# Reordering the opening of a fused FFT-filter and ELU kernel: weight fetches, table loads and on-chip weight conversion in another order

**Chip, cores, metric.** One core of one Trainium2 chip. The metric is the device time of one execution in microseconds (us); most executions of a kernel agree within 0.3%, which here is 8 us.

## The reference

```python
batch, seq, dim = (8, 3008, 256)
X = np.fft.rfft(x, axis=1)                        # x: 8 x 3008 x 256
y = np.fft.irfft(X * (filt_r + 1j * filt_i)[None], n=seq, axis=1)
h = y.reshape(24064, 256) @ w_in                  # 256 x 2048
g = np.where(h > 0, h, np.exp(np.minimum(h, 0)) - 1)
out = g @ w_out                                   # 2048 x 256
```

The weights reach the kernel as 64-bit floats. TensorE needs 32-bit ones, so the kernel converts them on the chip, in 16 pieces ("weights 0 to 15") of 0.52 MB each.

## The kernel before

The transforms are products with tables in three stages. In the kernel's words: `a_first` is the first stage on a chunk of x; `t_first` transposes; `b_unit` is the second stage of a frequency group and multiplies by the filter (four products on VectorE, lines 309 to 312); `bi_unit` is the first inverse stage, whose two results ScalarE copies (lines 329 and 330); `y_write` and `y_read` carry them through DRAM; `n_unit` is the last inverse stage (line 360), and `combine` (line 383) makes from it the operands of the first matrix product. After that the main part runs: 192 "quads" (8 batches x 6 blocks x 4 quarters of the hidden layer) on TensorE, each of two halves, with the FFT of the next batch woven in through a `plan` that hangs a function onto a half-quad. Only batch 0 has its FFT ahead of the main part, and so do the weights: that is the opening.

A weight is converted by two VectorE operations (`w_split`), four ScalarE operations (`w_float`), and three or four VectorE operations (`w_join`), every second time with four more that form sums.

```python
def w_split(k):
    m, e, c = wtmp[k % 2]                       # two sets of buffers
    ...
    nc.vector.tensor_scalar(out=m, in0=hi, scalar1=0x000FFFFF, ..., op0=ALU.bitwise_and)
    nc.vector.tensor_scalar(out=e, in0=hi, scalar1=0x7FF00000, ..., op0=ALU.bitwise_and)

def w_float(k):
    nc.scalar.activation(out=l, in_=wds[k][:, :, 0], func=AXT.Identity, ...)
    nc.scalar.activation(out=f, in_=m, func=AXT.Identity, ...)
    nc.scalar.activation(out=ef, in_=e, func=AXT.Relu, ...)
    nc.scalar.activation(out=e, in_=ef, func=AXT.Relu, ...)

# ---- the opening; NXC = 6 chunks of x, NG = 8 groups ----
TICKS = {0: 8, 1: 9, 3: 10, 5: 11, 7: 12, 8: 13, 9: 14}
f_arrange()                        # GpSimd's queue: filters rearranged, DRAM to DRAM
w_fetch(0, nc.sync)                # SyncE's queue
...
for c in range(NXC):
    x_load_first(c)                # SyncE's queue: chunk and its table
    if 0 < c < 5:
        w_fetch(c, nc.sync)
...
def tick(k):
    w_float(k)
    w_join(k - 1)

for c in range(NXC):
    w_split(c); w_float(c)
    a_first(c)
    if c > 0:
        w_join(c - 1)
        w_fetch(c + 4, nc.sync if c < 4 else nc.gpsimd)
nc.sync.dma_start(gs, gs_d)
for g in range(NG):
    f_read(0, g, ff[:, g])         # GpSimd's queue: filters to SBUF
    if g % 2:
        w_fetch(NXC + 4 + g // 2)  # w_fetch without a queue: GpSimd's
for g in range(4):
    t_first(g)
for k in (NXC, NXC + 1):
    w_split(k); tick(k); w_fetch(k + 8)
tn_read(0, 0)
for g in range(NG + 2):            # "the loop"
    k = TICKS.get(g)
    if k: w_split(k)
    if 2 <= g < NG - 2: t_first(g + 2)
    if g >= 2: bi_unit(0, g - 2)
    if g < NG: b_unit(0, g, ff[:, g], ...)
    if g >= 2: y_write(0, g - 2, (nc.sync, nc.scalar if g == NG + 1 else nc.sync))
    if g == NG + 1: y_read(0, 0, (nc.sync, nc.scalar))
    if k: tick(k)
w_split(15); tick(15)
w_join(15)
...
n_unit(0, 0)
# ---- main part: ----
for f in fbufs:                    # three filter buffers cleared together
    at(4, 1, nc.vector.memset, f, 0.0)
```

## Time and profile before

| | before |
|---|---|
| time, median of 4 runs | 2666.57 us (2664.87 to 2666.93) |
| profiled execution, span | 2665.7 us |
| TensorE busy | 2601.9 us (98%) |
| TensorE without work | 63.8 us: 51.2 up to `combine`, 4.3 in four waits behind it, 8.3 behind the last matmul |
| last chunk of x reaches TensorE | 46.3 us |
| first filter product (VectorE) | 62.8 us |
| first block enters the main part (`combine`) | 123.3 us |

The main part is the same work in both kernels and TensorE fills it. So the table to read is that of milestones in the opening. The lines are in the prediction.

The timeline of the kernel before, columns: start, length in us, engine, line, operation, tiles, idle time ahead of it and what ended it.

```profile
26.84 0.59 POOL L564 DMA_DIRECT2D wd<-in_moe_w_in_dram  x1 [0.37 <-issue]
31.69 0.55 POOL L564 DMA_DIRECT2D wd<-in_moe_w_in_dram  x1 [4.26 <-PE psa L250]
```

They are the fetches of weights 8 and 9, which start on GpSimd's queue while chunks of x are still on their way on SyncE's.

### The profile page before, as it was taken

What the parts mean: (1) busy time and instruction counts of PE and PEld (TensorE: products, weight loads), DVE (VectorE), ACT (ScalarE), POOL (GpSimd) and SP (SyncE); (2) the same over time, 40 slices, a digit from 0 to 9 for tenths busy, and PEclk for the clock granted to TensorE, in tenths of its full rate; (3) what the DMA queues carried; (4) which work ended last, traced back from release to release, by engine and by line L of the source; (5) the groups of instructions that cost most, each with busy time, mean ns of one, the idle gap of its engine ahead of it and who ended that gap; (6) DMA issues with size and microseconds to landing.
All of it is one profiled execution on the core that took longest, in us unless ns stands there. A gap on an engine that the chain in (4) does not pass through costs nothing.

```text
span 2665.7 us, 37335 instructions
## 1 busy us (share of the span) xinstructions
PE 2601.9 (98%) x13508; PEld 2213.2 (83%) x13508; DVE 1843.9 (69%) x3203; ACT 1507.8 (57%) x2622; POOL 235.6 (9%) x295
## 2 busy tenths in 40 slices
PE   4799999999999999999999999999999999999998
PEld 3388889888898878988889878898789888899887
DVE  4876767767676776767766776676767677666766
ACT  5555555555555555555555555555555555555554
POOL 4000200012000120002100021000210012000000
PEclk7799999999999999999999999999999999999999
DMA  9533411343124231333314242133421233110010
GB/s 277 129 94 92 109 44 38 92 107 94 38 51 123 77 86 38 86 97 80 78 41 102 73 99 74 38 85 96 105 56 38 68 87 87 39 40 19 21 28 17
DMA packets 224712, 202.85 MB, mean 76 GB/s; under 512 B 127586, under 2 KB 191090, under 8 KB 224528
## 3 DMA queue, kind: packets, MB, share of 16 engines
q1 hardware_dynamic: 212064, 167.23, 25.1%
q0 software_dynamic: 11008, 32.52, 4.7%
q8 instruction: 107, 1.75, 0.3%
q10 hardware_dynamic: 1456, 0.72, 0.1%
q14 instruction: 77, 0.63, 0.1%
HBM read 128.52 MB, written 74.97 MB: 76 GB/s over the span
## 4 chain that ended last, share of the span: by engine, by line
PE 95%; DMA 2%; DVE 1%; issue 0%; ACT 0%; SPq 0%; DVEq 0%; ACTq 0%
PE po L490 43%; PE phs L408 25%; PE phd L408 12%; PE pha L408 6%; PE psn L360 3%; PE pva L297 2%; PE psr L297 2%; PE psa L209 2%; DMA f<-in_moe_w_in_dram 1%; DMA xc<-in_x_dram 1%; PE pvb L297 1%; DMA wd<-in_moe_w_out_dram 0%; PE psi L297 0%; PE po L269 0%; DMA t<-yd 0%
## 5 line engine op out<-in xcount | busy, mean ns | idle before, releaser
L490 PE MATMUL po<-g,wo 128*128 128x256 f32 (+1 forms) x5376 | 1296.7, 375 | 0.0
L490 PEld LDWEIGHTS po<-g,wo 128*128 128x128 f32 x5376 | 1015.0, 190 | 129.5 <-issue 16.2
L419 ACT ACTIVATE g<-phs 128x512 f32<-128x512 f32 (+1 forms) x576 | 338.9, 588 | 844.2 <-PE phs L408 843.6
L416 DVE TENSOR_TENSOR g<-phd,g 128x512 f32<-128x512 f32 (+1 forms) x384 | 259.6, 676 | 463.7 <-ACT e L426 278.0
L426 ACT ACTIVATE e<-e 128x512 f32<-128x512 f32 (+1 forms) x768 | 477.3, 621 | 24.4
L408 PE MATMUL phs<-y,wi 128*128 128x256 f32 (+1 forms) x1536 | 395.1, 380 | 0.0
L408 PE MATMUL phs<-ys,wi 128*128 128x256 f32 (+1 forms) x1536 | 387.6, 375 | 2.5 <-ACT g L419 1.5
L430 DVE SCALAR_TENSOR_TENSOR g<-e,g 128x512 f32<-128x512 f32 (+1 forms) x576 | 387.1, 672 | 0.2 <-ACT e L426 0.2
L425 ACT ACTIVATE e<-g 128x512 f32<-128x512 f32 (+1 forms) x576 | 352.9, 613 | 35.4 <-DVE g L416 29.3
L408 PEld LDWEIGHTS phs<-y,wi 128*128 128x128 f32 x1536 | 284.9, 190 | 83.2 <-ACT t L329 34.1
L408 PEld LDWEIGHTS phs<-ys,wi 128*128 128x128 f32 x1536 | 291.4, 190 | 36.4 <-ACT g L419 2.2
L430 DVE SCALAR_TENSOR_TENSOR g<-e,phs 128x512 f32<-128x512 f32 (+1 forms) x192 | 130.0, 677 | 139.2 <-ACT e L426 139.2
L408 PE MATMUL phd<-ys,wi 128*128 128x256 f32 (+1 forms) x768 | 193.9, 375 | 1.8 <-DVE g L416 1.8
L408 PE MATMUL pha<-y,wi 128*128 128x256 f32 (+1 forms) x768 | 193.7, 375 | 0.0
L408 PE MATMUL phd<-y,wi 128*128 128x256 f32 (+1 forms) x768 | 193.7, 375 | 0.0
L425 ACT ACTIVATE e<-phs 128x512 f32<-128x512 f32 (+1 forms) x192 | 112.9, 588 | 141.4 <-PE phs L408 140.6
L318 POOL TENSOR_TENSOR sr<-sr,sp 128x512 f32<-128x512 f32 x56 | 71.1, 1270 | 1256.2 <-DVE sp L311 1256.2
L408 PEld LDWEIGHTS phd<-ys,wi 128*128 128x128 f32 x768 | 145.7, 190 | 18.9 <-DVE g L416 2.5
L408 PEld LDWEIGHTS pha<-y,wi 128*128 128x128 f32 x768 | 145.8, 190 | 16.5
L408 PEld LDWEIGHTS phd<-y,wi 128*128 128x128 f32 x768 | 145.8, 190 | 16.5
L467 DVE TENSOR_TENSOR g<-g,g 128x512 f32<-128x512 f32 (+1 forms) x192 | 130.7, 681 | 6.6
L470 DVE TENSOR_TENSOR g<-g,g 128x512 f32<-128x512 f32 (+1 forms) x192 | 130.7, 681 | 6.7
(134 smaller groups left out, 2393.1 us busy)
## 6 DMA issues: line engine op xcount, KB each, us to landing
yd<-t SPq DMA_DIRECT2D x127, 192.0 KB
t<-yd SPq DMA_DIRECT2D x190, 128.0 KB
z<-t SPq DMA_DIRECT2D x84, 256.0 KB
f<-fd POOLq DMA_DIRECT2D x112, 192.0 KB, 3.6
t<-z SPq DMA_DIRECT2D x224, 96.0 KB
out_dram<-o SPq DMA_DIRECT2D x632, 32.0 KB
tn<-tn_t SPq DMA_DIRECT2D x48, 256.0 KB
xc<-in_x_dram SPq DMA_DIRECT2D x84, 128.0 KB
```

Of the source, the lines that this page charges most:

```text
L297: nc.tensor.matmul(ps[:, u:u + w, :], table[k, v, :], r[k, u:u + w, :], start=n == 0, stop=n == len(rhs) - 1)
L318: nc.gpsimd.tensor_tensor(out=sr, in0=sr, in1=p, op=ALU.add)
L360: nc.tensor.matmul(ps[:, ts(q, P)], t[:, i - 4 * m, ds(dh * P, P)], w[:, i - 4 * m, :], start=True, stop=True)
L408: nc.tensor.matmul(ps[:, a, 0:h], w_in[q][:, COMBO[n], a, :], y[n], start=start and a == 0, stop=True, skip_group_check=True)
L416: nc.vector.tensor_tensor(out=g[o], in0=i0, in1=i1, op=ALU.add)
L419: nc.scalar.activation(out=g[o], in_=i0, func=AXT.Copy)
L425: nc.scalar.activation(out=e, in_=src, func=AXT.Relu, scale=-1.0)
L426: nc.scalar.activation(out=e, in_=e, func=AXT.Exp, scale=-1.0)
L430: nc.vector.scalar_tensor_tensor(out=g[n], in0=es[n], scalar=1.0, in1=src, op0=ALU.subtract, op1=ALU.max)
L467: nc.vector.tensor_tensor(out=b12, in0=b22, in1=b12, op=ALU.subtract)
L470: nc.vector.tensor_tensor(out=g["t4"], in0=g["b21"], in1=g["t2"], op=ALU.subtract)
L490: nc.tensor.matmul(po[i][:, u, 0:h], w_out[q][:, COMBO[n], a, :], g[n][:, a, :], start=q == 0 and a == 0 and n in (1, 3, 6, 4), stop=True, ...
```

## The change

The intent: x and the filters should not compete with weights that are needed late, and a conversion should never stand ahead of a filter product on VectorE or of the last copies on ScalarE. So:

- weights 1 to 3 go first on GpSimd's queue, ahead of the filter rearrangement; SyncE's queue carries only weights 0, 4 and 5 up to x's last chunk, and the tables (`once`, `gs`) follow x at once;
- no weight leaves on GpSimd's queue between the rearrangement and the first filter reads;
- a conversion (`step`) follows a step's products instead of framing them;
- `w_float(12)` is issued behind the last two pairs of copies;
- weight 15 is converted within the first three quads of the main part;
- the three clears are spread over quads 3 to 5.

```diff
-        elif k in (6, 7, 8, 9, 15):
+        elif k in (6, 7, 8, 9):                      # weight 15 in a filter buffer
...
-        if j % 2 == 1:
-            w = (w_in if j < 2 else w_out)[q]
+        if j % 2 == 1 and k < 15:
+            w_sums(k)                                # the four sums, cut out as a function
...
+            for k in (1, 2, 3):
+                w_fetch(k)
             f_arrange()
             w_fetch(0, nc.sync)
...
-            for c in range(NXC):
+            for c in range(3):
                 x_load_first(c)
-                if 0 < c < 5:
-                    w_fetch(c, nc.sync)
+            w_fetch(4, nc.sync)
...
+            def step(k):
+                w_split(k)
+                w_float(k)
+                if k > 0:
+                    w_join(k - 1)
+
+            for k in range(3):
+                step(k)
+            w_fetch(5, nc.sync)
+            for c in range(3, NXC):
+                x_load_first(c)
             nc.sync.dma_start(once, once_d)
-            def tick(k): ...
-            for c in range(NXC): ...
-            nc.sync.dma_start(gs, gs_d)
+            nc.sync.dma_start(gs, gs_d)
+            a_first(0)
+            w_fetch(6, nc.sync)
+            step(3)
+            for c in (1, 2):
+                a_first(c)
+                w_fetch(c + 6, nc.sync)
+            step(4)
+            a_first(3)
+            w_fetch(9, nc.sync)
+            step(5)
+            for c in (4, 5):
+                a_first(c)
+            tn_read(0, 0)
             for g in range(NG):
                 f_read(0, g, ff[:, g])
-                if g % 2:
-                    w_fetch(NXC + 4 + g // 2)
+                if 3 <= g < 5:
+                    w_fetch(g + 7)
+            for k in (12, 13):
+                w_fetch(k)
             for g in range(4):
                 t_first(g)
-            for k in (NXC, NXC + 1): ...
             for g in range(NG + 2):
-                k = TICKS.get(g)
-                if k:
-                    w_split(k)
...
-                if k:
-                    tick(k)
-            w_split(15)
-            tick(15)
-        w_join(15)
+                if g < 6:
+                    step(g + 6)
+                    if g == 0:
+                        w_fetch(14)
+                if g == 7:
+                    w_join(11)
+                    w_split(12)
+            w_float(12)
+            y_read(0, 0, (nc.sync, nc.scalar))
+            step(13)
+            w_fetch(15)
+            step(14)
+        w_join(14)
...
+        for quad, place, fn in ((0, 0, w_split), (0, 1, w_float), (1, 1, w_join), (2, 1, w_sums)):
+            at(quad, place, fn, 15)
...
-        for f in fbufs:
-            at(4, 1, nc.vector.memset, f, 0.0)
+        for i, f in enumerate(fbufs):
+            at(3 + i, 1, nc.vector.memset, f, 0.0)
```

More of the change, by code (lines that the diff above doesn't have):

```diff
@@ L552, in w_fetch @@
             wd = t1p.tile([P, XC, D], FP32, tag="t1", name="wd").rearrange("p u d -> p (u d)")
-        elif k in (6, 7, 8, 9, 15):
+        elif k in (6, 7, 8, 9):
             wd = xp.tile([P, 2, 2, D], FP32, tag="xc", name="wd").rearrange("p k u d -> p (k u d)")
         else:
-            wd = fbufs[{5: 0, 12: 1, 13: 2, 14: 0}.get(k, k)].rearrange("p c u d -> p (c u d)")
+            wd = fbufs[{5: 0, 12: 1, 13: 2, 14: 0, 15: 1}.get(k, k)].rearrange("p c u d -> p (c u d)")
         wd = wds[k] = wd.bitcast(U32).rearrange("p (a w) -> p a w", w=2)
@@ L571, in w_split @@
     def w_split(k):
-        m, e, c = wtmp[k % 2]
+        m, e, c = wtmp[k % 2 if k < 15 else 0]
         f, l = c[:, 0], c[:, 1]
@@ L606, in w_join, with w_sums @@
                 nc.vector.tensor_tensor(out=dst[:, i], in0=f[:, i], in1=e[:, i], op=ALU.mult)
-        if j % 2 == 1:
-            w = (w_in if j < 2 else w_out)[q]
-            a11, a21, a12, a22, s1, s2, s4 = (w[:, i] for i in range(7))
-            nc.vector.tensor_tensor(out=s1, in0=a21, in1=a22, op=ALU.add)
-            nc.vector.tensor_tensor(out=s2, in0=s1, in1=a11, op=ALU.subtract)
-            nc.vector.tensor_tensor(out=s4, in0=a12, in1=s2, op=ALU.subtract)
-            nc.vector.tensor_tensor(out=a21, in0=a11, in1=a21, op=ALU.subtract)
+        if j % 2 == 1 and k < 15:
+            w_sums(k)
+    def w_sums(k):
+        q, j = divmod(k, 4)
+        w = (w_in if j < 2 else w_out)[q]
+        a11, a21, a12, a22, s1, s2, s4 = (w[:, i] for i in range(7))
+        nc.vector.tensor_tensor(out=s1, in0=a21, in1=a22, op=ALU.add)
+        nc.vector.tensor_tensor(out=s2, in0=s1, in1=a11, op=ALU.subtract)
+        nc.vector.tensor_tensor(out=s4, in0=a12, in1=s2, op=ALU.subtract)
+        nc.vector.tensor_tensor(out=a21, in0=a11, in1=a21, op=ALU.subtract)
     def f_arrange():
@@ L634 @@
     with tc.manual_schedule():
-        TICKS = {0: 8, 1: 9, 3: 10, 5: 11, 7: 12, 8: 13, 9: 14}
         with tc.tile_pool(name="boot", bufs=1) as bp:
@@ L663 @@
                 nc.vector.memset(edges[:, i:i + 1], v)
-            nc.sync.dma_start(once, once_d)
-            def tick(k):
-                w_float(k)
-                w_join(k - 1)
-            for c in range(NXC):
-                w_split(c)
-                w_float(c)
-                a_first(c)
-                if c > 0:
-                    w_join(c - 1)
-                    w_fetch(c + 4, nc.sync if c < 4 else nc.gpsimd)
-            nc.sync.dma_start(gs, gs_d)
+            def step(k):
[8 more added lines that the diff above has]
+                x_load_first(c)
+            nc.sync.dma_start(once, once_d)
+            nc.sync.dma_start(gs, gs_d)
[3 more added lines that the diff above has]
+            for c in (1, 2):
+                a_first(c)
+                w_fetch(c + 6, nc.sync)
[6 more added lines that the diff above has]
+            tn_read(0, 0)
             for g in range(NG):
                 f_read(0, g, ff[:, g])
-                if g % 2:
-                    w_fetch(NXC + 4 + g // 2)
+                if 3 <= g < 5:
+                    w_fetch(g + 7)
+            for k in (12, 13):
+                w_fetch(k)
             for g in range(4):
                 t_first(g)
-            for k in (NXC, NXC + 1):
-                w_split(k)
-                tick(k)
-                w_fetch(k + 8)
-            tn_read(0, 0)
             for g in range(NG + 2):
-                k = TICKS.get(g)
-                if k:
-                    w_split(k)
                 if 2 <= g < NG - 2:
@@ L700 @@
                     y_write(0, g - 2, (nc.sync, nc.scalar if g == NG + 1 else nc.sync))
-                if g == NG + 1:
-                    y_read(0, 0, (nc.sync, nc.scalar))
-                if k:
-                    tick(k)
-            w_split(15)
-            tick(15)
-        w_join(15)
+                if g < 6:
[11 more added lines that the diff above has]
+        w_join(14)
         for c in range(2):
```

## The prediction

> **What bounds the kernel now.** I read the page's slices first, then a table of busy time by stretch, then the chain of waits and the timeline of the opening.
>
> ```profile
> PE   4799999999999999999999999999999999999998
> DMA  9533411343124231333314242133421233110010
> ...
> 0.00:57.00 57.00, 25.96 (x140) 24.00 (x144) 23.13 (x45) 30.51 (x58) 28.52 (x56) 0.73 1.01 283
> 57.00:106.00 49.00, 40.99 (x230) 16.42 (x222) 41.40 (x82) 29.58 (x52) 5.06 (x9) 0.76 0.52 131
> 106.00:118.00 12.00, 0.00 (x0) 0.00 (x0) 9.39 (x21) 6.33 (x11) 0.00 (x0) 0.61 0.47 122
> 118.00:132.00 14.00, 12.27 (x56) 10.93 (x56) 11.14 (x24) 8.06 (x16) 0.00 (x0) 0.84 0.93 215
> ...
> 400.00:2600.00 2200.00, 2200.00 (x11411) 1888.59 (x11410) 1531.93 (x2648) 1250.62 (x2172) 173.11 (x197) 1.00 0.28 69
> ```
>
> The columns of the table are length, then PE, PEld, DVE, ACT and POOL busy, granted clock, DMA share and GB/s. From 195 to 2600 us TensorE is never idle at full clock: the change doesn't touch that work. TensorE busy is 2601.9 of 2665.7 us, so all that any reordering can win is 64 us of idle time, and nearly all of it lies before 132 us. There are three stretches. Up to 57 us all 16 DMA engines are full (share 1.01). From 57 to 106 us VectorE is busy 41.4 of 49 us (filter products of the first batch, with weight conversion between them). From 106 to 118 us TensorE waits for the first batch's round trip through DRAM.
>
> ```profile
> 46.28 3.76 PE L250 MATMUL psa<-t,x 128*128 128x128 f32 x16 [7.44 <-DMA x<-in_x_dram]
> ...
> 62.83 0.68 DVE L309 TENSOR_TENSOR sr<-psr,ff 128x512 f32<-128x512 f32 x1
> ...
> 107.53 0.63 ACT L583 ACTIVATE wfl<-wm 128x512 f32<-128x512 uint32 x1 [2.16 <-DVE wm L576]
> ...
> 109.43 0.58 ACT L329 ACTIVATE t<-pva 128x512 f32<-128x512 f32 x1
> ...
> 118.17 3.75 PE L360 MATMUL psn<-tn,t 128*128 128x128 f32 x16 [12.62 <-DMA t<-yd]
> ...
> 123.34 0.38 DVE L383 TENSOR_TENSOR ys<-y 128x224 f32<-128x224 f32 x1
> ```
>
> These are the milestones. The last chunk of x arrives at 46.3. The first filter product, whose matmuls ended at about 57.7, starts only at 62.8, because the join of weight 5, all of weight 6 and the split of weight 7 are ahead of it on VectorE. The last bi_unit's matmuls end at 105.5, but ScalarE copies them at 109.4: a conversion of weight 13 stands ahead and itself waits for VectorE. The first combine of the second half starts at 123.3, behind VectorE's joins of weights 14 and 15.
>
> ```profile
> q0 software_dynamic: 3666, 9.96, 52.1%
> q1 hardware_dynamic: 4784, 9.44, 49.0%
> ...
> PE phd L408 <- DVE g L416: 1.8, 1, 1.8
> ```
>
> The first two lines are the queues in the first 70 us: GpSimd's and SyncE's transfers share the engines evenly. The third, from TensorE's waits of 118 to 300 us, is the one stall that the three clears of the filter buffers cause (at 185 to 188 us on VectorE); after 300 us there is no wait at all.
>
> **What the Trainium skill says.** "DMA: Bandwidth & Descriptors", section "Queues, rings and completion order": each DMA engine takes turns between queues that have work, packet by packet. The trace agrees (52.1% against 49.0%). Its section "Issuing engines are not separate DMA queues" says that issuing from several engines saves only issue time; so moving weights 1 to 3 to GpSimd's queue changes the order of landing and not the rate, which is 283 GB/s here. "TensorE: Matmul & The Clock Gate", Part 1: the clock is halved after an idle window of about 3.4 us and restored after a busy one. The trace agrees: the granted clock is 0.50 from 20 to 50 us, and a 48x512 matmul of line 297 takes 1.06 us near 68 us and 0.59 near 102 us. Same page, on queue depths ("Architectural detail"): ScalarE and VectorE take instructions strictly in order, as the 109.4 us copy shows.
>
> **The change part by part.** No matmul, product or weight byte is removed. What moves is this.
>
> *x earlier.* Up to x's last chunk SyncE's queue carried weights 0 to 4; now it carries 0, 4 and 5. At 0.52 MB a weight that is 1.57 MB of weights, 3.1 of x and 1.5 of tables, 6.2 MB in place of 7.3. The old 7.3 MB took 46.1 us, 158 GB/s, so x should land at 6.2/0.158 = 39 us, 7 us earlier. From its first matmul (46.28) to b_unit(0)'s first (56.2) were 10 us, so b_unit(0) could run at about 49.
>
> *Filters later.* GpSimd's queue first takes weights 1 to 3, 1.57 MB. At half of 283 GB/s that is 11 us. The filter rearrangement ended at about 33 us, when the first filter read was let go (33.55), so it now ends near 43. The first read (0.39 MB) needs 3 us at half rate and some 3 of latency: the filters are there at 49 to 52. That takes about 3 us of the 7. In return GpSimd's filter reads no longer stand behind weights 6 to 9, which waited for chunk buffers.
>
> *Products first.* With both, and no conversion ahead on VectorE, I put the first product at 52 us in place of 62.8: 11 us won.
>
> *The loop.* On VectorE a group of four products takes 2.4 us (62.83 to 65.22), a split 0.68, a join 2.0 to 2.1, and with its sums 3.7 (65.22 to 68.93). Between the first product and the last now stand six splits (4.1), joins 5 to 10 (3 x 3.7 + 3 x 2.07 = 17.3) and eight groups (19.2): 40.6 us. Before, the same stretch (62.83 to 103.4) took 40.5 with 33.6 of work and 7.0 idle for TensorE. The loop therefore carries more work now. With a conversion behind each group TensorE can prepare the next during it; of the idle time I keep 3 us. That is 43.6, so the last product ends at about 96 (before 103.4): 7.4 of the 11 us remain.
>
> *The last copies.* The last matmuls end 2.1 us after the products (105.5 - 103.4), now at 98; with nothing ahead on ScalarE the two copies end at 99.2. The way from the last copy's end (110.5) to the first matmul of n_unit (118.17) is two transfers, 7.7 us; so 106.9. From there to the combine were 5.2 us: 112.1. VectorE by itself: from 96 join 11 (3.7), splits 12 and 13 (1.4) to 101; join 12 (2.1), split 14 (0.7), join 13 (3.7) and join 14 (2.1), with ScalarE's four activations per weight (2.6 us) between, end at about 112. The two paths meet, at 112.3 against 123.3: **11 us won**.
>
> *Weight 15 and the clears.* Weight 15 moves into the first three quads of the main part. VectorE has room, but ScalarE's 2.6 us stand at the end of quad 0, ahead of the copy that quad 1's second accumulation needs. TensorE waited 0.9 us for that copy already; I charge 2 us. The clears, one to a quad now in quads 3 to 5, should save the 1.8 us stall. Net 0.2 lost.
>
> Sum: 2666.3 - 11.0 + 0.2 = 2655.5, rounded to 2656.
>
> **The rivals.** *TensorE becomes the bound of the loop.* A step costs it about 3.8 us at full clock (bi_unit 2.0, b_unit 0.9, transposes 0.9) and 7.6 at half, against some 6 us of VectorE. For it: the clock of 57 to 106 us was 0.76 on average, and every slow patch there ended in VectorE waiting for TensorE. Against: a TensorE that is the bound is busy, and warms up. All six steps cold would add 9 us (2665); half of them 4.
>
> *The filters are the bound.* If rearranging, whose transfers are small, suffers more than in proportion from starting behind the weights, the first reads land near 57 and all shifts by 5 us: 2661. For it: at most eight transfers of a queue are open, and each took about 7 us to land. Against: once x is in, GpSimd's queue has the engines nearly alone.
>
> *Hidden anyway.* VectorE's total before the main part falls only by weight 15 (3.7 us), and if every product that comes early just waits for the joins at the end, only that and idle time are won: about 4 us, 2662. Against: between the first product and the combine VectorE's work grows by one join and one split only (joins 5 to 14 in place of 7 to 15), some 3 us, and about 10 of the 60.5 us there were idle.
>
> *Better than reckoned.* x at 37, filters at 46, TensorE warm: 6 us more, 2649.
>
> **Range and chances.** The first product is uncertain by about 3 us, the loop by 4, the end by 2; together some 5, with the failures tending later. I give 2649 to 2663. Faster by over 2% would need 53 us of the 64 us of idle time in all; slower by as much would need a stall that nothing here suggests. Within 2%: 0.99.
>
> **What would show it right or wrong.** In the profile after: x's last chunk matmul at 38 to 42 us (before 46.3); first product 49 to 55, with the wait ahead of it on a filter read or on TensorE; groups of products 5.5 to 7 us apart; copies of pva directly behind the last matmuls; n_unit at 105 to 109; the combine at 110 to 115; no stall at the clears, and a wait of 2 to 3 us for a copy in quad 1. The prediction is wrong if the first product is later than 57, if the loop takes over 50 us, if joins 13 and 14 end several us after n_unit's copies, or if TensorE, idle-free before from 195 us on, shows waits there.

## The result, and the profile after

| | before | after |
|---|---|---|
| time, median of 4 runs each | 2666.57 us | 2655.38 us (2652.79 to 2656.22) |
| profiled execution, span | 2665.7 us | 2651.0 us |

The ratio is 0.9958, with a 95% interval of 0.994 to 0.9975: 0.4% less time, and 0.6 us from the predicted time. All outputs are right. A ratio here is the mean time of one kernel's runs over that of the other's runs of the same rounds, so it is not quite the ratio of the medians quoted. The profiled execution of the changed kernel happened to be the fastest of its four runs, and that of the kernel before (2667.5 us) was slower than all its four, so the traces are 14.7 us apart while the medians are 11.2 apart.

The page's slices after the change:

```profile
PE   5799999999999999999999999999999999999998
...
DMA  9534311533134321423214342134321333110010
```

The first slice (66 us) rises from 4 tenths to 5; every later slice of TensorE is as before. The table by stretch after the change (columns as in the prediction: length; PE, PEld, DVE, ACT and POOL busy; clock; DMA share; GB/s):

```profile
0.00:57.00 57.00, 30.30 (x182) 25.24 (x182) 29.87 (x58) 34.27 (x63) 31.00 (x61) 0.86 1.00 297
57.00:106.00 49.00, 35.47 (x207) 18.37 (x206) 45.21 (x92) 33.18 (x58) 4.27 (x8) 0.81 0.62 162
106.00:118.00 12.00, 8.03 (x37) 6.66 (x36) 9.79 (x19) 8.29 (x16) 0.00 (x0) 0.92 0.77 184
118.00:132.00 14.00, 14.00 (x78) 12.69 (x78) 6.15 (x11) 7.38 (x14) 0.00 (x0) 0.82 0.32 86
```

Up to 57 us TensorE now works 30.3 us instead of 26.0, at the same DMA share. From 57 to 106 it is VectorE that gained, from 41.4 to 45.2 busy microseconds. And the stretch from 106 to 118, which had no matmul at all, has 8.0 us of them: the main part has begun. Queues in the first 70 us, after the change:

```profile
q0 software_dynamic: 3856, 10.49, 52.9%
q1 hardware_dynamic: 5184, 9.70, 45.8%
```

The two queues still share the engines about evenly: in 70 us GpSimd's moved 0.5 MB more than before and SyncE's 0.3. What changed is which transfer stands where. Then the milestones, in the timeline after the change:

```profile
35.97 6.22 PE L250 MATMUL psa<-t,x 128*128 128x128 f32 x32 [2.52 <-ACT we L586]
...
47.94 0.69 DVE L309 TENSOR_TENSOR sr<-psr,ff 128x512 f32<-128x512 f32 x1 [15.12 <-DMA ff<-fd]
...
92.16 0.59 ACT L330 ACTIVATE t<-pvb 128x512 f32<-128x512 f32 x1
...
93.25 0.68 ACT L582 ACTIVATE wfl<-f 128x512 f32<-128x512 uint32 x1 [0.50 <-DVE wo L617]
...
100.17 3.76 PE L360 MATMUL psn<-tn,t 128*128 128x128 f32 x16 [8.58 <-DMA t<-yd]
...
105.00 0.39 DVE L383 TENSOR_TENSOR ys<-y 128x224 f32<-128x224 f32 x1
...
116.59 0.52 ACT L419 ACTIVATE g<-phs 128x448 f32<-128x448 f32 x1
...
117.16 1.86 PE L408 MATMUL phs<-ys,wi 128*128 128x224 f32 x4 [3.34 <-ACT g L419]
```

The last two chunks of x now form one group of 32 matmuls from 35.97 us on. The last chunk has landed by 38.0 (SyncE's queue, which waited for that transfer, goes on then), and TensorE starts on it without a wait at about 39.5. The 38.0 compares with 46.3 before, where TensorE started as the chunk landed. The first product is at 47.9, and the bracket tells what it waited for: 15.1 us, ended by a filter read. The last copy starts at 92.2, and only after it comes the conversion of weight 12 (line 582 at 93.3). `n_unit` is at 100.2 and `combine` at 105.0. The last two lines are the price: in quad 1 TensorE waits 3.34 us for a ScalarE copy (line 419), which stood behind the four conversions of weight 15. TensorE's waits from 105 us on say the same in one line (columns: total us, times, longest):

```profile
PE phs L408 <- ACT g L419: 4.0, 2, 3.3
```

The wait for the clears, 1.8 us in the kernel before, is gone.

**The balance of the pair of traces.** `combine` is 18.3 us earlier (123.34 - 105.00). From `combine` to `n_unit` of the second block there were 19.37 us before (142.71 - 123.34), and there are 24.65 after (129.65 - 105.00): 5.3 us are given back in the first two quads. The clears return 1.8. 18.3 - 5.3 + 1.8 = 14.8, against a difference of spans of 14.7. Of the 5.3, the wait is 3.34 - 0.9 = 2.4. The rest is clock: the three groups of matmuls that follow the wait took 1.86, 3.19 and 1.49 us, where the same groups take 1.02, 1.68 and 0.92 at full clock, 2.9 us less. Told by idle time, the same 14.7 us are 10.8 us less of it and 3.9 us less of TensorE's busy time (2601.9 to 2598.0 us): the work of the opening itself ran at a higher clock, 0.86 against 0.73 up to 57 us.

### The profile page after: what moved, and what is told of

It is laid out like the page before. It is cut to its first block, busy times and chain, and to the rows that moved or that the text cites. A ratio compares the mean times of both kernels' runs of the same rounds, so it can differ in the third digit from the quotient of the medians.

```text
span 2651.0 us, 37333 instructions
## 1 busy us (share of the span) xinstructions
PE 2598.0 (98%) x13508; PEld 2213.7 (84%) x13508; DVE 1843.7 (70%) x3203; ACT 1507.5 (57%) x2622; POOL 236.3 (9%) x298
## 4 chain that ended last, share of the span: by engine, by line
PE 96%; DMA 2%; DVE 0%; ACT 0%; POOL 0%; issue 0%; DVEq 0%; SPq 0%; POOLq 0%
PE po L490 43%; PE phs L408 25%; PE phd L408 12%; PE pha L408 6%; PE psn L360 3%; PE pva L297 2%; PE psr L297 2%; PE psa L209 2%; DMA fd<-in_filt_i_dram 1%; DMA ff<-fd 1%; DMA wd<-in_moe_w_out_dram 0%; DMA fd<-in_filt_r_dram 0%; PE pvb L297 0%; DMA f<-in_moe_w_out_dram 0%; DMA t<-yd 0%
```

## The experiments

Questions: Which part of the change earns the gain? Is it the order of bytes on the queues, the place of the conversions, or the putting off of weight 15? And are the 5.3 us really weight 15's? Times below are medians over 5 rounds, each with "gain", the difference of mean times to the kernel before in the same call; the kernel before was at 2666.9, 2666.7, 2668.0 and 2667.1 us (medians of 9 runs) in the four calls. The calls ran on different chips. The changed kernel itself was run only in the first (experiments 1, 4, 7 and 8), where it gained 12.7 us; the others are compared with it through the kernel before, so differences of a few us between them and the changed kernel are weaker evidence.

### 1. The changed kernel again

No edit; the baseline.

> The changed kernel once more, as the yardstick of this call. My theory: the time hangs on whether TensorE's clock drops after the 3.3 us stall in quad 1 (behind weight 15's ScalarE work) and for how long, so 2652 to 2657 us, and the stall of 3 to 4 us shows in quad 1 again. Rival: the stall was an accident of one profile; then it is missing here and the time is the same.

Measured: 2654.69 us (2652.69 to 2655.35), ratio 0.9952 (0.9939 to 0.9966), gain 12.7. The trace repeats: first product 47.7, `combine` 104.8, the wait of 3.3 us in quad 1. So the stall and the early opening belong to the kernel, not to one execution.

### 2. The changed opening alone

The changed order up to the filter reads; the loop, its end, weight 15 ahead of the main part and the clears as before.

```diff
-            for g in range(NG + 2): ...   # changed loop: products, then step(g + 6)
+            for k in (NXC, NXC + 1):
+                w_split(k); tick(k); w_fetch(k + 8)
+            for g in range(NG + 2): ...   # the old loop with its TICKS, w_split(15), tick(15)
```

> The kernel before with the changed opening alone (order of the loads and of the first five conversions); loop, end, weight 15 and clears as before. My theory: x and filters allow the first product at 47 to 48 us, conversions 6 and 7 ahead of it put it at 52 to 54 (62.8 before); from there the old loop and end take 60.5 us as before, so the combine at 113 to 115 and 2656 to 2658 us, some 9 to 10 us faster than before. Rival (the order in the loop is what pays): the first product is early, but the old loop gives it back, 2662 or more.

Measured: 2654.77 us (2654.66 to 2656.14), ratio 0.9956, gain 11.6. Timeline of this kernel:

```profile
50.40 0.69 DVE L309 TENSOR_TENSOR sr<-psr,ff 128x512 f32<-128x512 f32 x1
...
110.59 0.39 DVE L383 TENSOR_TENSOR ys<-y 128x224 f32<-128x224 f32 x1
```

`combine` comes 12.75 us earlier than before, and the time gained is 11.6. **The opening by itself brings as much as the whole change.** (The edit holds the new order of the transfers and that of the first six conversions; this run doesn't part the two.) The first product has no wait ahead of it here: it stands behind the conversions that the old loop puts first, and starts only 2.5 us later than in the changed kernel.

### 3. The changed loop and end alone

The old opening, with everything else changed.

```diff
-            for k in (1, 2, 3): w_fetch(k)
...                                        # the old order up to the filter reads,
+            for c in range(NXC): ...      # with step() for the conversions of the loop
```

> The changed kernel with the opening of before (loads and first conversions), so the changed loop, end, weight 15 and clears alone. My theory: first product at about 57 us (matmuls of b_unit at 56), 41.5 us of loop and 15.6 to the combine, so the combine at 114 (123.3 before), less the stall at weight 15 (5 us) and plus the clears (1.8): 2659 to 2662 us. With the opening alone at -9 to -10 and this at -5 to -7, the parts add to more than the whole (-11.7), because both move the same conversions out of the way of the first product. Rival (the loop is the whole of it): 2656.

Measured: 2662.89 us (2662.53 to 2666.09), ratio 0.9988 (0.9976 to 1.0001), gain 3.0. Timeline:

```profile
59.41 0.69 DVE L309 TENSOR_TENSOR sr<-psr,ff 128x512 f32<-128x512 f32 x1 [8.14 <-PE psi L297]
...
119.42 0.39 DVE L383 TENSOR_TENSOR ys<-y 128x224 f32<-128x224 f32 x1
```

The first product gains 3.4 us without any earlier data, but now waits 8.1 us for TensorE. `combine` gains 3.9, and the first two quads, with the 3.3 us stall in quad 1 (it is in this trace too), give 4.1 back (23.50 us from `combine` to `n_unit` of the second block, against 19.37); the spread clears return 1.8. That is less than the 5 to 7 us expected. Together with experiment 2: the loop and the end bring `combine` forward by another 5.6 us on top of the new opening (110.6 to 105.0), but the stall costs 5.3 of them.

### 4. Weight 15 in smaller pieces

The four ScalarE conversions of weight 15 one to a half-quad, instead of four in a row at the end of quad 0.

```diff
-        for quad, place, fn in ((0, 0, w_split), (0, 1, w_float), (1, 1, w_join), (2, 1, w_sums)):
-            at(quad, place, fn, 15)
+        for quad, place, fn, a in ((0, 0, w_split, ()), (1, 0, w_float, ((0,),)), (1, 1, w_float, ((1,),)),
+                                   (2, 0, w_float, ((2,),)), (2, 1, w_float, ((3,),)),
+                                   (3, 0, w_join, ()), (3, 1, w_sums, ())):
+            at(quad, place, fn, 15, *a)      # w_float(k, parts): only these of the four
```

> Only weight 15's four ScalarE activations are moved: one at a time, in quads 1 and 2, in place of all four at the end of quad 0; join and sums in quad 3. My theory: the stall of 3.3 us in quad 1 goes, and with it the half clock that followed it (some 2 us more), so 4 to 6 us faster than the changed kernel: 2649 to 2651. Rival (the stall is the start-up of the pipeline, which the kernel before has too, with other waits): less than 1.5 us faster.

Measured: 2650.79 us (2649.43 to 2652.13), ratio 0.9937, gain 16.3: 3.6 us better than the changed kernel, a little less than the 4 to 6 expected. The table by stretch, first of the changed kernel, then of this one:

```profile
112.00:118.00 6.00, 2.66 (x12) 2.28 (x11) 5.28 (x10) 4.87 (x9) 0.00 (x0) 0.84 0.67 154
118.00:125.00 7.00, 7.00 (x35) 5.69 (x35) 1.06 (x2) 2.18 (x5) 0.00 (x0) 0.65 0.01 2
```

```profile
112.00:118.00 6.00, 5.10 (x28) 4.75 (x27) 5.36 (x11) 3.83 (x8) 0.00 (x0) 1.00 0.93 221
118.00:125.00 7.00, 7.00 (x48) 6.21 (x47) 3.74 (x7) 5.50 (x11) 0.00 (x0) 1.00 0.39 114
```

In the changed kernel TensorE is busy 2.66 of 6 us around the wait, and then runs 7 us at a mean clock of 0.65 with 35 matmuls. In pieces, it is busy 5.10 of 6, the clock stays at 1.00, and 48 matmuls fit into the same 7 us. The wait is back at 0.9. So the cause of the loss is shown: it is the row of four conversions, and about half of its cost is the clock that drops after the wait. The traces of the two kernels are 3.3 us apart: `combine` is 1.0 later in this one (105.86 against 104.82), the first two quads return all of the 5.3 (19.37 us again, against 24.71), and a new wait of 0.8 us appears, of TensorE for the sums of weight 15, which VectorE now makes later.

### 5. Weight 15 in two pieces

Two conversions at the end of quad 0, two at the end of quad 1, to see whether a shorter wait keeps the clock.

```diff
+        for quad, place, fn, a in ((0, 0, w_split, ()), (0, 1, w_float, ((0, 1),)), (1, 1, w_float, ((2, 3),)),
+                                   (2, 1, w_join, ()), (3, 1, w_sums, ())):
```

> The changed kernel with two of weight 15's four ScalarE activations left at the end of quad 0 and two moved to the end of quad 1. It tells the stall from the slow clock that follows it. My theory: ScalarE's work ahead of the copy falls by 1.3 us and the stall from 3.3 to 2.0; too short an idle time for the clock to drop (full clock from the stall on), so 3 to 5 us faster than the changed kernel, about as much as with all four spread, 2650 to 2652. Rival (the clock would have dropped in any case, only the stall counts): 1.3 us faster, 2653.5.

Measured: 2653.26 us (2652.72 to 2655.41), ratio 0.9949, gain 13.6. The wait is 1.98 us. The table by stretch of this kernel:

```profile
112.00:118.00 6.00, 4.02 (x21) 3.44 (x20) 5.16 (x10) 5.41 (x10) 0.00 (x0) 1.00 0.83 202
118.00:125.00 7.00, 7.00 (x39) 5.78 (x39) 2.27 (x4) 2.75 (x6) 0.00 (x0) 0.76 0.02 6
```

TensorE is busy 4.02 of 6 us, and yet the clock falls, to 0.76. My theory, that a wait this short leaves the clock alone, falls; the rival is right. The Trainium skill, "TensorE: Matmul & The Clock Gate", Part 1, puts the fall at an idle window of about 3.4 us. Here a wait of 1.98 us, with TensorE busy on both sides of it, was followed by a fall, so the measurement decides. But no length of wait follows from it as a limit. The clock did not fall in the wait: it stayed at 1.00 through it (115.8 to 117.75 us) and for 1.3 us of work more, then was 0.50 for 3.4 us with TensorE busy (119.1 to 122.5). And the clears' wait of 1.8 us in the kernel before, hardly shorter, left the clock alone:

```profile
190.00:195.00 5.00, 3.19 (x16) 2.53 (x15) 4.90 (x9) 3.47 (x7) 0.89 (x2) 1.00 0.64 157
195.00:200.00 5.00, 5.00 (x33) 4.61 (x32) 4.79 (x10) 2.14 (x4) 0.00 (x0) 1.00 0.00 0
```

The same is seen in the traces of experiments 2 and 10. So waits of 0.9 and 1.8 us did no harm here, and one of 2.0, in a single trace, did.

### 6. Weight 15 ahead of the main part

The changed kernel with weight 15 converted inline, as before.

```diff
             step(14)
-        w_join(14)
+            step(15)
+        w_join(15)
```

> The changed kernel with weight 15 converted ahead of the main part, as before, and not in quads 0 to 2. My theory: the combine comes 4 to 5 us later (109 to 110: split, 2.6 us of ScalarE, join and sums), and the stall of 3.3 us in quad 1 with the slow clock after it is gone (5 us), so within 1.5 us of the changed kernel's 2655: putting weight 15 off, as it was done, won nothing. Rival (putting it off hides it): 3 us or more slower.

Measured: 2658.36 us (2654.11 to 2659.25), ratio 0.9964, gain 9.4. This is about 3 us worse than the changed kernel (12.7, but on another chip, and the ranges of the runs overlap). `combine` is at 113.87, 8.9 us later; of these 4.3 are a loop that ran later (its last group of products starts at 91.31, against 87.01), which the edit doesn't touch, and 4.6 are the conversion (22.56 us from there to `combine`, against 17.99). TensorE's waits show what comes in place of the stall:

```profile
PE phs L408 <- DVE ys L385: 3.0, 1, 3.0
PE phs L408 <- ACT y L362: 2.3, 1, 2.3
```

TensorE now waits for the operands of the first block instead. The first two quads take 22.1 us in place of 24.7, so the edit itself costs about 2 us of the 6.5 between the traces. The later loop may belong to the chip or the execution: all three traces of the changed loop on this chip (experiments 3, 6 and 9) take 44.6 to 44.7 us from first to last product, against 41.5 in both of the changed kernel's. Whether putting weight 15 off pays in spite of the stall is therefore not decided.

### 7. A conversion ahead of each step's products

In the first six steps `step(g + 6)` goes ahead of `b_unit`. This undoes one point of the intent alone.

```diff
+                if g < 6:
+                    step(g + 6)
+                    if g == 0:
+                        w_fetch(14)
                 if g < NG:
                     b_unit(0, g, ff[:, g], gf, pq if g % 2 else None)
                 if g >= 2:
                     y_write(...)
-                if g < 6:
-                    step(g + 6)
-                    if g == 0:
-                        w_fetch(14)
```

> In each of the first six steps of the loop the conversion stands ahead of the filter products and not behind them. My theory: what counts is when VectorE's work is available, not that products come first; VectorE was idle for 15.1 us up to the first filter read, so the first conversion (split 6 and join 5, 4.4 us) fits into that gap and the rest of the order is unchanged; the first product stays at 47 to 49 us, the combine comes 3 to 4.5 us earlier, total 2651. Rival (the change's intent: products first pays): the first product comes 3 to 5 us later and the total is 2656 to 2660.

Measured: 2651.15 us (2649.47 to 2653.66), ratio 0.9940, gain 15.7: 3.0 us *better* than the changed kernel. Timeline:

```profile
48.83 0.69 DVE L309 TENSOR_TENSOR sr<-psr,ff 128x512 f32<-128x512 f32 x1 [3.58 <-DMA ff<-fd]
...
82.62 0.69 DVE L309 TENSOR_TENSOR sr<-psr,ff 128x512 f32<-128x512 f32 x1 [2.62 <-PE psi L297]
...
104.28 0.38 DVE L383 TENSOR_TENSOR ys<-y 128x224 f32<-128x224 f32 x1
```

The conversion fills time in which VectorE waited for the filters anyway: the wait ahead of the first product shrinks from 15.1 us to 3.6, and the product is 0.9 us later only. "Products first" therefore does not pay at the start of the loop. But the time saved shows poorly in the milestones: TensorE's later steps do not keep up (VectorE waits 2.62 and 1.26 us for it), and `combine` is earlier by 0.5 to 0.7 us. Where the 3.0 us of time come from is not settled. The profiled pair is 1.8 us apart (2650.9 and 2649.1): 0.5 is the earlier `combine`, and 1.2 lie in the first two quads, where after the same wait of 3.3 us the half clock lasted 3.5 us in place of 6.8 (mean 0.83 against 0.65 from 118 to 125 us). Nothing in the edit explains that, and among traces with the same wait both occur (0.65 to 0.83), so this part may be chance.

### 8. Both together

The edits of 4 and 7.

> Both edits of this call together. My theory: they act in different places, so the gains add: 8 us faster than the changed kernel, 2646 to 2648. Rival for either: only the other one's gain is seen, 2650 to 2652.

Measured: 2648.11 us (2645.49 to 2650.2), ratio 0.9927 (0.9914 to 0.9939), gain 19.1. **This is the best version**: it beats the kernel before by 19 us and the changed kernel by 6.4. `combine` is at 104.61, the clock stays at 1.00 from 112 to 132 us, and TensorE's waits in quad 1 are 0.9 us or less.

### 9. A conversion ahead of the last copies

`w_float(12)` right behind `w_split(12)` in the loop, so ScalarE meets it ahead of the last two pairs of copies.

```diff
                     w_join(11)
                     w_split(12)
-            w_float(12)
+                    w_float(12)
```

> The changed kernel with weight 12's ScalarE work put ahead of the last two bi_units' copies (as a conversion stood there before). My theory: those copies wait for VectorE's split 12 (94 us) and 2.6 us of activations, 96.7 in place of 91.7 to 92.2; the round trip through DRAM starts 4 to 5 us later and the combine comes at 109 to 110 (105.0): 3 to 5 us slower than the changed kernel, 2658 to 2660. Rival (VectorE's joins end at the same time anyway, so the copies are hidden): less than 1.5 us slower.

Measured: 2663.74 us (2662.03 to 2664.85), ratio 0.9989, gain 3.1. Measured through the kernel before, it costs 8 to 10 us, where I had expected 3 to 5; the rival, that the wait is hidden, falls. Timeline:

```profile
96.87 0.63 ACT L583 ACTIVATE wfl<-wm 128x512 f32<-128x512 uint32 x1 [6.52 <-DVE wm L576]
...
115.86 0.39 DVE L383 TENSOR_TENSOR ys<-y 128x224 f32<-128x224 f32 x1
```

ScalarE stands 6.5 us in front of one conversion, because VectorE has not yet made its input, with finished matmul results behind it. The Trainium skill, "TensorE: Matmul & The Clock Gate", "Architectural detail", calls ScalarE's queue strictly first in, first out, and the trace agrees: the two pairs of copies behind it leave at 98.8 to 100.8 us in one go. The last copy ends at 100.8 instead of 92.75. Of these 8 us, 3.3 are a later loop in this execution (as in experiment 6) and 4.7 the conversion; so the edit itself costs some 6 of the 9.3 us between the traces. Then a second cost joins in: the last two writes of y take 5.7 us to land, where the last took 3.1 in the changed kernel. They leave together now, but the fetch of weight 15 (0.52 MB) also runs beside them, which in the changed kernel started after y had landed. Which of the two makes the 5.7 us is not shown.

### 10. The clears together again

```diff
-        for i, f in enumerate(fbufs):
-            at(3 + i, 1, nc.vector.memset, f, 0.0)
+        for f in fbufs:
+            at(4, 1, nc.vector.memset, f, 0.0)
```

> The changed kernel with the three clears of the filter buffers back together in quad 4. My theory: TensorE's wait of 1.8 us for VectorE in quad 4 is back, and the total is 1.5 to 2 us longer than the changed kernel's, 2656 to 2657 us. Rival: with weight 15's work no longer near, VectorE absorbs the clears and the wait is not there; total the same as the changed kernel's.

Measured: 2656.32 us (2654.34 to 2657.87), ratio 0.9957, gain 11.3. The time does not resolve it: 0 to 1.4 us worse than the changed kernel. The waits do:

```profile
PE phd L408 <- DVE g L416: 1.8, 1, 1.8
```

The same line as in the kernel before is back, with the same 1.8 us. That is all that spreading the clears is worth; the clock stays at 1.00 after this wait.

### 11. Weights 1 to 3 on SyncE's queue again

They go between the chunks of x, as before; all else stays changed. SyncE's queue then carries some 7.7 MB up to x's last chunk, more than in the kernel before.

```diff
-            for k in (1, 2, 3):
-                w_fetch(k)
...
             for c in range(3):
                 x_load_first(c)
+                w_fetch(c + 1, nc.sync)
```

> The changed kernel with weights 1 to 3 back on SyncE's queue, each behind a chunk of x, everything else as changed. My theory: 1.57 MB more ahead of x's last chunk put it at 46 to 48 us (38 in the changed kernel); filters arrive some 8 us earlier but wait; the first product at 56 to 58, all 8 to 10 us later, total 2662 to 2665. Rival (both queues share the same engines, so the queue doesn't matter): first product within 3 us of 48, total 2655 to 2658.

Measured: 2654.32 us (2652.46 to 2656.08), ratio 0.9952, gain 13.0. No difference to the changed kernel. The first product in the timeline:

```profile
48.17 0.69 DVE L309 TENSOR_TENSOR sr<-psr,ff 128x512 f32<-128x512 f32 x1 [12.22 <-PE psi L297]
```

It is 0.2 us later than in the changed kernel, and now it is TensorE that it waited for, so x, and not the filters: the filter reads are let go at 34.6 us instead of 41.8, and x's last chunk is there at 40.8 instead of 38.0. The two paths tie within about a microsecond, and which queue carries weights 1 to 3 trades one for the other. **My theory falls here**, and with it a step of the prediction: had x moved at the old 158 GB/s of its queue, it would have come at 7.7 MB / 0.158 = 49 us. It came at 40.8, at 190 GB/s. So what makes x early is not mainly how much its own queue carries; that is worth these 2.8 us.

### 12. Two weights beside x's last chunks

What is left is what runs beside x. This kernel is number 11 with weights 12 and 13 (1.05 MB), which are needed late, moved forward on GpSimd's queue to just behind the filter rearrangement. No byte is added.

```diff
             step(3)
+            for k in (12, 13):
+                w_fetch(k)
             for c in (1, 2):
...
-            for k in (12, 13):
-                w_fetch(k)
```

> The kernel of the last run (weights 1 to 3 on SyncE's queue; there x's last chunk landed at about 40.8 us and the first product came at 48.2) with one more edit: GpSimd's queue fetches weights 12 and 13, 1.05 MB, right behind the filter rearrangement, so that they run beside x's last chunks, as weights 8 to 10 do in the kernel before. My theory, now that which queue carries weights 1 to 3 has turned out not to matter: the changed opening is faster because no large weights compete with x at the end, so here x's last chunk lands 2.5 to 4 us later (43.5 to 45), the filter reads too, the first product comes at 51 to 53, and the total is 2 to 4 us longer, 2656 to 2658. Rival (SyncE's queue moves at its own rate whatever GpSimd's carries): last chunk and first product within 1 us of the last run, total the same, 2654.

Measured: 2663.92 us (2661.67 to 2668.24), ratio 0.9992, gain 3.0. Timeline:

```profile
29.85 0.58 POOL L564 DMA_DIRECT2D f<-in_moe_w_in_dram  x1 [1.97 <-DMA f<-in_moe_w_in_dram]
30.73 0.54 POOL L564 DMA_DIRECT2D f<-in_moe_w_in_dram  x1 [0.29 <-DMA fd<-in_filt_i_dram]
...
46.67 3.75 PE L250 MATMUL psa<-t,x 128*128 128x128 f32 x16 [5.19 <-DMA x<-in_x_dram]
...
56.06 0.69 DVE L309 TENSOR_TENSOR sr<-psr,ff 128x512 f32<-128x512 f32 x1 [20.01 <-PE psi L297]
```

Two fetches issued at 29.9 and 30.7 us put x's last chunk back to 46.7, where it was before the change, and the first product to 56.1; the gain falls by some 10 us. That is more than expected, in the delay of x (2.5 to 4 us expected) and in the time. This is the pattern of the kernel before, with its weights 8 and 9 at 26.8 and 31.7. The gain left, 3.0 us, is that of experiment 3, which has the changed loop on the old opening. **So it is shown that the opening earns its gain by keeping large transfers away from x's last chunks.** The delay is larger than the bytes: 1.05 MB are an estimated 3.7 us at the 283 GB/s of this stretch, and x came 5.9 us later. The other 2 us stay open. The reverse, the kernel before with only weights 8 to 10 kept away from x, was not run.

## Why the prediction was right

The total was right: 2656 predicted, 2655.4 measured, within the range. Point by point it was partly right: errors of opposite sign cancelled, and that part is luck.

- **x earlier: the time right, the reason wrong.** Predicted 39 us, measured 38.0. The step divided the bytes on SyncE's queue by that queue's old rate. Experiment 11 put those bytes back and x came at 40.8, and experiment 12 undid the gain with transfers on the other queue. What set the old rate were the weights beside x. That 39 met 38.0 is luck.
- **Filters later: right.** Predicted release of the reads near 43 and their landing at 49 to 52; measured 41.8, and the first product at 47.9 waited for a filter read. (Its own sum was 43 + 3 + 3 = 49; the 52 used below is the late end of its range.) The text named the weights wrongly: the reads had stood behind weights 8 and 9, with 10 and 11 between them, not behind 6 to 9; nothing rested on it.
- **Products first: mis-sized.** Predicted first product at 52, measured 47.9, 4.1 us better. Conversions ahead of it did cost in the kernel before: with nothing earlier on the queues, the changed loop brings it forward by 3.4 us (experiment 3), and the old loop on the new opening puts it back by 2.5 (experiment 2). In the changed kernel one conversion ahead costs 0.9 (48.8 in experiment 7), because VectorE waits for filters anyway.
- **The loop: 2.1 us too long.** Predicted 43.6 us from first to last product, measured 41.5 (47.94 to 89.5). I kept 3 us of idle time; VectorE idled 1.26. In other kernels with the same loop it idled 3.0 (experiment 11) and 4.2 (experiment 9), so this is also chance.
- **The last copies: right.** Copies directly behind the matmuls, 7.4 us from the last copy to `n_unit` (7.7 predicted), both paths meeting at `combine`: y's copy ends at 104.5 and VectorE's joins at 105.0. Experiment 9 shows the cost of the opposite, and it is larger than I thought.
- **Weight 15: mis-sized.** Charged 2 us, measured 5.3, because I counted the wait (3.34, of which 0.9 was there) but not the 2.9 us of reduced clock behind it.
- **The clears: right**, 1.8 us in the waits.
- **"All that any reordering can win is 64 us of idle time, nearly all of it before 132 us": wrong in both halves.** 52.8 of the 63.8 us lie before 132 us and 8.3 behind the last matmul, and 3.9 of the 14.7 us won in the traces are busy time that ran at a higher clock. The total does not rest on it.

In the sum, `combine` was 7.3 us earlier than predicted (105.0 against 112.3: 4.1 from the first product, 2.1 from the loop, 1.1 from the end). Weight 15 took 3.3 of these back, and the executions that were not profiled were some 3 us slower than the profiled one. Of the rivals, "TensorE becomes the bound of the loop" came true only in its small form (waits of 1 to 4 us); "the filters are the bound" was right about which wait ends last and wrong about the size; "hidden anyway" falls with experiment 2. "Better than reckoned" is what the milestones did.

Open are: where the 3.0 us of experiment 7 come from, 2 of the 5.9 us in experiment 12, the 5.7 us of the writes in experiment 9, and whether putting weight 15 off pays when it is not cut into pieces (experiment 6).

## What to carry to other kernels

For a load that everything waits for, ask what lands *beside* its last part, on any queue, before asking what its own queue carries; hold late data back until that part is in. Work that is put off onto an in-order engine within a full main part must be cut into pieces shorter than the slack of the copy behind it, for a wait can cost its own length once more in clock. And check a prediction that came true step by step: here two wrong terms cancelled, and the repair of one of them (experiment 4) brought 3.6 us on top of a gain of 12.7.

## What the Trainium skill lacked or had wrong

- "TensorE: Matmul & The Clock Gate", Part 1, ties the lower clock to an idle window of about 3.4 us. Here it fell after single waits of 1.98 us (TensorE busy 4.02 of 6 us, mean clock then 0.76 over 7 us) and of 3.34 us (busy 2.66 of 6, 0.65), and did not after 0.9 us (busy 5.10 of 6, 1.00) or after 1.81 us (busy 3.19 of 5, 1.00, in three traces). After the 1.98 us it fell only 1.3 us later, in the middle of work. The page's "A second HAM failure mode" speaks of short idle times without a length; these numbers could stand there.
- "DMA: Bandwidth & Descriptors", "Issuing engines are not separate DMA queues", agrees with experiment 11 (2654.32 us against 2654.69 with three weights on the other queue). It does not say what a transfer beside a critical load costs: 1.05 MB started about 11 us ahead of the last chunk's landing delayed the last chunk by 5.9 us and the first product by 7.9.
- No page that I read says how much of the engines is left to one queue while the other does small rearranging transfers: SyncE's queue moved 7.7 MB in 40.8 us (190 GB/s) beside them, and 7.3 MB in 46.1 us (158 GB/s) with 0.52 MB weights beside it.
